# Mixture-of-experts chunks on one Trainium2 core: transposes set between products, and one bank exchanged

## The chip, the cores and the metric

The kernel runs on one core of a Trainium2 chip. The metric is the time on the device in microseconds, from the first to the last instruction plus what lies around them. The core's engines each run an instruction stream of their own and wait for each other through counters (semaphores): TensorE (PE in the rows; PEld are its weight loads), VectorE (DVE), ScalarE (ACT), GpSimd (POOL), and SyncE (SP), which issues most DMAs.

## The reference

Windowed attention gives 1536 rows of 512; a dense layer pair (2048 inner values) follows, then a gated layer of eight experts. Only the last is touched by the change:

```python
    expert_idx = np.argmax(logits, axis=1)          # E = 8 experts, N = 1536 tokens
    ...                                             # a token's place in its expert; capacity 384
    h = np.maximum(np.einsum('ecd,edf->ecf', disp, w1), 0.0)      # D = 512 -> F = 1024
    y = np.einsum('ecf,efd->ecd', h, w2)                          # F = 1024 -> D = 512
    ...
            out[i] = gate_w[i] * y[expert_idx[i], pos[i]]
```

With the inputs used here the experts get 715, 147, 16, 240, 4, 20, 277 and 117 tokens.

## The kernel before, in words

The order on every engine is the order in which the code is written (the schedule is manual). Attention, the dense pair and the routing take the first 420 us. The experts follow. An expert's tokens are handled in chunks of 128 rows, up to three (`NCH`), named (expert, chunk) below: (3,1) is the second chunk of expert 3. Chunk 0 of each expert always runs. Chunks 1 and 2 stand in nested conditionals (`guard`, `further_chunks`, L1310 to L1329), which each engine decides by a count that it reads itself. With these counts six further chunks run: (0,1), (0,2), (1,1), (3,1), (6,1), (6,2). Experts 2, 4, 5 and 7 skip theirs. An engine that skips a conditional raises its counter in one step by all that the body would have counted, and does so when its own earlier instructions are finished (the `EVENT_SEMAPHORE` of L1327 in the profile).

A chunk has four parts. All products are made of three matmuls, since every operand is split into a high and a low part (float32r).

- `turn_in` (L422): four transposes of the token rows into one PSUM bank, a copy to the high part on ACT (`xh`), a subtraction for the low part on DVE (`xl`).
- `expert_up` (L1253): two halves of 512 inner values, each 12 matmuls (128x512) into a bank of its own, and then the Relu of the half on ACT into `hh` (L1267).
- `turn_hidden` (L1270): for each half four transposes of `hh` (L1282), a copy to the high part on ACT (`hth`, L1285), a subtraction to the low part on DVE (`htl`, L1286). Between the two halves `between` transposes the tokens of the chunk after this one.
- `expert_down` (L1290): 24 matmuls over the eight blocks of inner values (high, high, low for each block), a scaling on DVE (`yo`, L1305), and a scatter by POOL.

The eight PSUM banks go round in three sets: three for transposes (`t`, rows name them es), three for `expert_up` (`u`, et), two for `expert_down` (`y`, et and eo). Each chunk (run or not) takes its banks when the program is built.

Weights for later experts are converted meanwhile: `expert_split` makes the high part by an ACT copy of 128x1024 (L1196, 1.05 to 1.07 us) and the low part by a DVE subtraction (L1197, 1.22 us). The loop over experts sets their places, and for experts of at least 1 it runs: `expert_up(e, 0)`, `turn_in(e + 1, 0)`, `turn_in(e, 1)`, splits, `expert_down(e - 1, 0)` (from expert 2 on), `turn_hidden(e, 0)`, further splits, `further_chunks(e, 1)`.

Of the kernel before, what the change touches and what calls it, by code (L numbers as in the profile page):

```python
# [9 lines left out]
F32 = mybir.dt.float32  # L10
F32R = mybir.dt.float32r
# [3 lines left out]
AF = mybir.ActivationFunctionType  # L15
ALU = mybir.AluOpType
# [19 lines left out]
def attention_mlp_moe_kernel(  # L36
# [17 lines left out]
    nc = tc.nc  # L54
    P = 128
    B, _, _, S = q.shape
    _, NG, _, GH, NQ, D1 = v.shape
# [4 lines left out]
    E = w_gate.shape[2]  # L62
    F = w1.shape[2]
    KD = DM // P
    KF = DFF // P
    KE = F // P
# [4 lines left out]
    if n_sink == 0 and window == 0:  # L71
# [4 lines left out]
    NCH = -(-max(1, min(capacity, NT)) // P)  # L76
# [8 lines left out]
    ident = const.tile([P, P], F32, name="ident")  # L85
# [6 lines left out]
        out=lt, in_=lt, pattern=[[1, P]], compare_op=ALU.is_gt, fill=0.0,  # L92
# [28 lines left out]
    def slot(tag, dt=F32R):  # L121
        slot_n[tag] = slot_n.get(tag, 0) + 1
        return slot_pool[tag].tile([P, SW], dt, tag=tag, name=f"{tag}_{slot_n[tag]}", bufs=1)
# [7 lines left out]
    for bl in range(NT // XB):  # L131
        for kp in range(KD // 2):
            for hl in range(2):
                t = slot(f"x{(bl * (KD // 2) + kp) * 2 + hl}")
# [167 lines left out]
    def spots(nb, seg):  # L302


        o = ns if nb == 1 and seg else 0
        offs = [o + n * BS for n in range(nb)]
        return offs, (0 if nb == 1 else P), offs[-1] + P
# [99 lines left out]
    three = ((0, 0), (0, 1), (1, 0))  # L407
# [5 lines left out]
    rows, tx, ep = {}, {}, []  # L413
# [9 lines left out]
    def turn_in(e, c, pt=None, th=None, tl=None):  # L423
        r = rows.pop((e, c))
        if pt is None:
            tag = "a" if c == 0 else "b"
            pt = next_bank("t")
            th = ep[0].tile([P, DM], F32R, tag=f"xh{tag}", name=f"xh{e}_{c}", bufs=1 + (c > 0))
            tl = ep[0].tile([P, DM], F32R, tag=f"xl{tag}", name=f"xl{e}_{c}", bufs=1 + (c > 0))
        for kk in range(KD):  # L430
            nc.tensor.transpose(pt[:, kk * P:(kk + 1) * P], r[:, kk * P:(kk + 1) * P], ident)
        nc.scalar.copy(th, pt)
        nc.vector.tensor_sub(tl, pt, th.bitcast(F32))
        tx[e, c] = (th, tl)
# [187 lines left out]
    with ExitStack() as actx:  # L622
# [12 lines left out]
        for n in range(QA):  # L635
            t = ap_c.tile([P, 2, S], F32, name=f"qa{n}")
# [5 lines left out]
        for i in range(NQ):  # L642
# [4 lines left out]
            offs, so, w = spots(len(row), seg)  # L647
# [4 lines left out]
            for (d, sink), o in zip(row, offs):  # L652
# [3 lines left out]
                if d * P - (P - 1) < 0:  # L656
                    nc.gpsimd.affine_select(
                        out=mb, in_=mb, pattern=[[-1, P]], compare_op=ALU.is_ge,
                        fill=NEG, base=d * P, channel_multiplier=1,
                    )  # L660
                if d * P + (P - 1) > window - 1:
                    nc.gpsimd.affine_select(
                        out=mb, in_=mb, pattern=[[1, P]], compare_op=ALU.is_ge,
# [9 lines left out]
        if small:  # L673
            for n in range(3):
                t = ap_c.tile([P, 2, 4, D1], F32, name=f"vsk{n}")
                nc.gpsimd.memset(t, 0.0)
                vsks.append(t)
                t = ap_c.tile([P, P], F32, name=f"pk{n}")
# [190 lines left out]
        for b in range(B):  # L869
            for hp in range(H // 2):  # L870
# [3 lines left out]
                for i0 in range(0, NQ, 2):  # L874
                    t = Item()
                    t.st, t.n, t.nm, t.units = st, len(groups), f"{st.nm}_{i0}", []
                    for ii in range(min(2, NQ - i0)):
                        u = Item()
# [32 lines left out]
        def at(xs, n):  # L911
            return xs[n] if 0 <= n < len(xs) else None
# [23 lines left out]
        for n in range(nu + 11):  # L936
            u = at(units, n)
# [36 lines left out]
            if n == nu - EARLY:  # L974
                nc.vector.tensor_scalar(
                    out=nalpha, in0=alpha_sb, scalar1=-1.0, scalar2=None, op0=ALU.mult
# [196 lines left out]
    experts = {}  # L1173
# [29 lines left out]
    def splits_to(n):  # L1203
        while split_n[0] < min(n, len(raw_src)):
            if split_n[0] == raw_n[0]:
                raw_loads()
            expert_split(split_n[0])
            split_n[0] += 1
# [27 lines left out]
    def next_bank(nm):  # L1236
        n = bank_n[nm] = bank_n.get(nm, -1) + 1
        return banks[nm][n % len(banks[nm])]
# [3 lines left out]
    counts, hid, hts = {}, {}, {}  # L1242
# [4 lines left out]
    def guard(e, c):  # L1247
        if e not in counts:
            counts[e] = nc.values_load(  # L1249
                cnt_i[0:1, e:e + 1], engines=GE, min_val=0, max_val=NT  # L1250
            )
        return tc.If(counts[e] > c * P)

    def expert_up(e, c):
        ups = experts[e][0]
        x = tx.pop((e, c))
        h = ep[0].tile([P, F], F32, tag="hh", name=f"hh{e}_{c}", bufs=1)
        for o in range(0, F, 512):
            ph = next_bank("u")
            for kk in range(KD):  # L1260
                for n, (xl, wl) in enumerate(((0, 0), (0, 1), (1, 0))):
                    nc.tensor.matmul(  # L1262
                        ph, x[xl][:, kk * P:(kk + 1) * P],
                        ups[kk][wl][:, o:o + 512],
                        start=(kk == 0 and n == 0), stop=(kk == KD - 1 and n == 2),
                    )
            nc.scalar.activation(h[:, o:o + 512], ph, AF.Relu)  # L1267
        hid[e, c] = h

    def turn_hidden(e, c, between=None):  # L1270
        h = hid.pop((e, c))


        tag = "b" if (c > 0) != (e == E - 1) else "a"
        th = ep[0].tile([P, F], F32R, tag=f"hth{tag}", name=f"hth{e}_{c}", bufs=1)
        tl = ep[0].tile([P, F], F32R, tag=f"htl{tag}", name=f"htl{e}_{c}", bufs=1)
        hts[e, c] = (th, tl)
        for o in range(0, F, 512):
            w = slice(o, o + 512)
            pt = next_bank("t")  # L1280
            for j in range(o // P, o // P + 4):
                nc.tensor.transpose(  # L1282
                    pt[:, j * P - o:(j + 1) * P - o], h[:, j * P:(j + 1) * P], ident
                )
            nc.scalar.copy(th[:, w], pt)  # L1285
            nc.vector.tensor_sub(tl[:, w], pt, th.bitcast(F32)[:, w])  # L1286
            if o == 0 and between:
                between()

    def expert_down(e, c):  # L1290
        downs = experts[e][1]
        ht = hts.pop((e, c))
        py = next_bank("y")
        n = e * NCH + c
        y = ep[0].tile([P, DM], F32, tag="yo", name=f"yo{n}", bufs=1)
        for j in range(KE):
            for x, (hl, wl) in enumerate(((0, 0), (0, 1), (1, 0))):
                nc.tensor.matmul(
                    py, ht[hl][:, j * P:(j + 1) * P], downs[j][wl],
                    start=(j == 0 and x == 0), stop=(j == KE - 1 and x == 2),  # L1300
                )
        if n == (E - 1) * NCH:
            nc.scalar.activation(y, py, AF.Copy, scale=meta[:, n, 0:1])
        else:
            nc.vector.tensor_scalar(  # L1305
                out=y, in0=py, scalar1=meta[:, n, 0:1], scalar2=None, op0=ALU.mult
            )
        nc.gpsimd.indirect_dma_start(  # L1308
            out=out[:, :], out_offset=bass.IndirectOffsetOnAxis(ap=token[:, n:n + 1], axis=0),
            in_=y, in_offset=None, bounds_check=NT - 1, oob_is_err=False,  # L1310
        )

    def further_chunks(e, c):

        if c == NCH:
            return
        if NCH > 3:
            for c in range(1, NCH):
                with guard(e, c):
                    if c > 1:  # L1320
                        fetch(e, c)
                        turn_in(e, c)
                    expert_up(e, c)
                    turn_hidden(e, c)
                    expert_down(e, c)
            return
        with guard(e, c):  # L1327
            expert_up(e, c)
            turn_hidden(e, c, (lambda: turn_in(e, c + 1)) if c + 1 < NCH else None)  # L1329
            expert_down(e, c)  # L1330
            further_chunks(e, c + 1)

    nc.gpsimd.dma_start(
        out=meta, in_=xs.rearrange("(n p) d -> p n d", p=P)[:, :, DM:XW]
# [4 lines left out]
    for e in range(E):  # L1339

        splits_to((e + 1) * PER - (e == 1))
        if e:
            expert_up(e, 0)
        raw_loads()
        if 0 < e < E - 1:
            turn_in(e + 1, 0)
        if e and NCH > 1:
            turn_in(e, 1)
        fetch(e + 2, 0)
        fetch(e + 1, 1)  # L1350
        splits_to((e + 1) * PER)
        raw_loads()
        splits_to((e + 1) * PER + PW1 + 1 * (e == 0) - (e == 1))
        if e == E - 1:
            turn_hidden(e, 0)
        if e >= 2:
            expert_down(e - 1, 0)
        if 0 < e < E - 1:
            turn_hidden(e, 0)
        if e == E - 1:  # L1360
            expert_down(e, 0)
        raw_loads()
        splits_to((e + 1) * PER + PW1)
        raw_loads()
        if e == 0:
            more = nc.values_load(more_i[0:1, 0:1], engines=GE, min_val=0, max_val=P)
            with tc.If(more > 0):
                turn_in(0, 0)
                expert_up(0, 0)
                turn_hidden(0, 0)  # L1370
                expert_down(0, 0)
            turn_in_slot(1, 0, "r4", next_bank("y"))
        further_chunks(e, 1)
        if NCH == 3:
            fetch(e + 1, 2)
# [64 lines left out]
```

## Time and profile before

| | |
|---|---|
| time, median of 3 runs | 606.62 us (605.58 to 607.24) |
| profiled execution | 605.23 us, of which the span from first to last instruction is 603.4 us |
| PE busy | 580.9 us, 96% of the span |
| DVE, ACT, POOL busy | 419.8, 346.6, 83.8 us |
| mean granted TensorE clock | 0.996 of full speed |

A timeline row gives the start of a group of instructions, its duration, engine, line, operation, output and inputs, tile shape and count; in brackets stands the idle time of the engine just before it and what ended that. Matmuls overlap, so the pace is read from one start to the next and not from the durations.

### The profile page before, as it was taken

To read this page: it belongs to the slowest core of one execution; us is meant where nothing else is said; L and a number is where in the kernel's file an instruction comes from. 1 tells how busy PE (TensorE), PEld (TensorE's weight loads), DVE (VectorE), ACT (ScalarE), POOL (GpSimd) and SP (SyncE) were. 2 spreads that over 40 slices of the span, in tenths; PEclk is the share of its full clock that TensorE was granted. 3 is DMA by queue.
4 is the path that set the end of the run, shared out by engine and by line. 5 is a ranking of instruction groups with operands and counts; after the bars stand their busy time and mean duration, and the time that the engine had idled before them with its cause. 6 is when DMAs were issued, how large, how long until landed. Compare 5 with 4: busy or idle time off the path is not lost. (4 is left out here: it accounts for less than half of the span.)

```text
span 603.4 us, 9071 instructions
## 1 busy us (share of the span) xinstructions
PE 580.9 (96%) x3174; PEld 485.2 (80%) x3174; DVE 419.8 (70%) x872; ACT 346.6 (57%) x641; POOL 83.8 (14%) x128
## 2 busy tenths in 40 slices
PE   7999999999989999999999999999999999999994
PEld 6999998878767888888899898976777777778783
DVE  6578878689999568974577787965326783885240
ACT  5677776566565545444466677854238474775330
POOL 5011433210000000000200021113210211111011
PEclk9999999999999999999999999999999999999998
DMA  7969742224641660000100022334918692993000
GB/s 226 329 209 307 209 142 71 71 70 145 200 146 68 216 272 2 0 1 0 54 19 2 0 78 74 113 110 136 348 45 295 216 380 102 348 356 127 18 21 35
DMA packets 32996, 83.86 MB, mean 139 GB/s; under 512 B 3646, under 2 KB 4206, under 8 KB 32944
## 3 DMA queue, kind: packets, MB, share of 16 engines
q1 hardware_dynamic: 28800, 71.66, 35.6%
q0 software_dynamic: 4144, 11.53, 5.5%
q8 instruction: 30, 0.49, 0.3%
q14 instruction: 22, 0.18, 0.1%
HBM read 68.75 MB, written 16.31 MB: 141 GB/s over the span
## 5 line engine op out<-in xcount | busy, mean ns | idle before, releaser
L362 PE MATMUL h<-x,r 128*128 128x512 f32 (+1 forms) x768 | 148.6, 340 | 3.2 <-DVE r L274 3.1
L362 PEld LDWEIGHTS h<-x,r 128*128 128x128 f32 x768 | 120.5, 189 | 22.8 <-DVE r L274 5.2
L393 PE MATMUL acc<-r,gh 128*128 128x512 f32 x384 | 120.5, 395 | 0.0
L393 PEld LDWEIGHTS acc<-r,gh 128*128 128x128 f32 x384 | 69.9, 188 | 14.2
L393 PE MATMUL acc<-r,gl 128*128 128x512 f32 x192 | 75.9, 395 | 0.0
L736 PE MATMUL s<-ka,qa 128*128 128x260 f32 x192 | 59.9, 399 | 4.2 <-DMA qa<-in_q_dram 3.9
L846 PEld LDWEIGHTS o<-vr,pT 128*128 128x128 f32 x352 | 55.5, 192 | 4.8
L375 DVE SCALAR_TENSOR_TENSOR g<-gn,nalpha,g 128x512 f32<-128x512 f32 (+1 forms) x64 | 39.4, 615 | 24.3 <-ACT g L374 24.2
L274 DVE TENSOR_TENSOR r<-wo,r 128x1024 fp32r<-128x1024 f32 x31 | 37.9, 1224 | 24.7 <-ACT r L271 24.5
L373 ACT ACTIVATE gn<-h 128x512 f32<-128x512 f32 (+1 forms) x64 | 31.4, 491 | 40.8 <-PE h L362 40.3
L846 PE MATMUL o<-vr,pT 128*128 128x65 f32 x352 | 53.6, 251 | 0.0
L1267 ACT ACTIVATE hh<-et 128x512 f32<-128x512 f32 x26 | 15.6, 599 | 65.5 <-PE et L1262 59.2
L1153 POOL DMA_INDIRECT xs<-x,slot_i x12 | 14.4, 1198 | 264.3 <-ACT g L374 164.4
L382 ACT CAST gh<-g 128x512 fp32r<-128x512 f32 (+1 forms) x64 | 32.9, 514 | 28.1 <-DVE g L375 27.9
L755 ACT ACTIVATE p<-sx,mn 128x260 f32<-128x260 f32 (+1 forms) x96 | 42.9, 488 | 9.4 <-DVE mn L751 8.9
L271 ACT CAST r<-wo 128x1024 fp32r<-128x1024 f32 (+1 forms) x33 | 33.8, 1025 | 22.6 <-PE acc L393 21.7
L768 PE MATMUL pt<-ident,p 128*128 128x128 f32 x176 | 46.5, 279 | 0.0
L751 DVE CUSTOM_DVE_ANT_0 sx<-s,mask 128x260 f32<-128x260 f32 (+1 forms) x96 | 36.9, 400 | 13.7 <-PE s L736 9.7
L393 PEld LDWEIGHTS acc<-r,gl 128*128 128x128 f32 x192 | 36.1, 188 | 8.6
L274 DVE TENSOR_TENSOR r<-wi,r 128x1024 fp32r<-128x1024 f32 x30 | 36.7, 1222 | 2.3 <-ACT r L271 2.3
L385 DVE TENSOR_TENSOR gl<-g,gh 128x512 fp32r<-128x512 f32 (+1 forms) x64 | 35.4, 553 | 1.6 <-ACT gh L382 1.6
L736 PEld LDWEIGHTS s<-ka,qa 128*128 128x128 f32 x192 | 30.9, 200 | 5.2 <-issue 3.8
(204 smaller groups left out, 1101.5 us busy)
## 6 DMA issues: line engine op xcount, KB each, us to landing
raw_all<-in_w_dram SPq DMA_DIRECT2D x36, 512.0 KB, 5.7
more_raw<-in_w_dram SPq DMA_DIRECT2D x28, 512.0 KB, 6.3
raw_all<-in_w_in_dram SPq DMA_DIRECT2D x8, 1024.0 KB, 6.3
raw_all<-in_w_out_dram SPq DMA_DIRECT2D x8, 1024.0 KB, 5.0
xs<-r SPq DMA_DIRECT2D x8, 771.0 KB, 10.1
rows<-xs POOLq DMA_DIRECT2D x20, 256.0 KB, 5.8
vr<-in_v_dram SPq DMA_DIRECT2D x4, 780.0 KB, 5.0
out_dram<-fill SPq DMA_DIRECT2D x2, 1536.0 KB, 13.2
```

Source lines behind the costliest of these rows:

```text
L271: nc.scalar.copy(hi[:, x], w[:, x])
L274: eng.tensor_sub(lo[:, x], w[:, x], hi.bitcast(F32)[:, x])
L362: nc.tensor.matmul(ph[:, :TB], wi[wl][:, kk, f0:f0 + P], xT_at(kk, tok, TB, xl), start=(n == 0), stop=(n == 3 * KD - 1),)
L375: nc.vector.scalar_tensor_tensor(out=g, in0=gn, scalar=nalpha[:, f:f + 1], in1=g, op0=ALU.mult, op1=ALU.add)
L382: nc.scalar.copy(gh, g)
L385: nc.vector.tensor_sub(gl, g, gh.bitcast(F32))
L393: nc.tensor.matmul(acc[t], g[a][:, t * P:(t + 1) * P], wo[w][:, f % FG, :], start=(f == 0 and x == 0), stop=(f == KF - 1 and x == 2),)
L736: nc.tensor.matmul(s[:, o:o + w], st.qa[:, h, toks], st.ka[:, c:c + w], start=True, stop=True, skip_group_check=True,)
L751: nc.vector.tensor_tensor_reduce(out=x[:, :w], in0=u.s[h][:, :w], in1=m[:, :w], scale=-scale, scalar=BIG, op0=ALU.add, op1=ALU.min, accum_ ...
L755: nc.scalar.activation(t.p[:, u.ii, h, :w], x[:, :w], AF.Exp, bias=t.mn[:, c:c + 1], scale=-1.0)
L768: nc.tensor.transpose(pt[:, c * P:(c + 1) * P], t.p[:, u.ii, h, u.offs[n]:u.offs[n] + P], ident,)
L846: nc.tensor.matmul(t.o[:, 2 * u.ii + h, :], u.pT[:, w], vr[:, hv * NQ + j, :], start=(not sg and n == 0), stop=(n == len(js) - 1), skip_gr ...
```

## The change

Three edits. First, a further chunk's work goes into one function, `chunk_alone`, which writes PE's instructions in another order: the transposes of the first half stand between the two halves of the second half's 12 `expert_up` matmuls, and the transposes of the second half stand after the first six `expert_down` matmuls. Second, the Relu of the second half is made in two pieces of 256 columns, one on ACT and one on DVE. Third, expert 1's `turn_in(1, 1)` takes a `y` bank in place of a `t` bank. Chunk 0 of every expert keeps the old functions; `put_out` is the end of `expert_down` under a name of its own.

```diff
@@ chunk_alone, new; further_chunks calls it for expert_up, turn_hidden, expert_down
+        mid = KD // 2
+        for o in cuts:
+            ph = next_bank("u")
+            up(o, ph, range(mid))
+            if o:
+                turn(o - 512)
+            up(o, ph, range(mid, KD))
+            if o < cuts[-1]:
+                nc.scalar.activation(h[:, o:o + 512], ph, AF.Relu)
+            else:
+                nc.scalar.activation(h[:, o:o + 256], ph[:, :256], AF.Relu)
+                nc.vector.tensor_scalar(
+                    out=h[:, o + 256:o + 512], in0=ph[:, 256:], scalar1=0.0, scalar2=None,
+                    op0=ALU.max,
+                )
+        if between:
+            between()
+        py = next_bank("y")
+        n = KE // 4
+        down(range(n))
+        turn(cuts[-1])
+        down(range(n, KE))
+        put_out(e, c, py)
...
-            expert_up(e, c)
-            turn_hidden(e, c, (lambda: turn_in(e, c + 1)) if c + 1 < NCH else None)
-            expert_down(e, c)
+            chunk_alone(e, c, (lambda: turn_in(e, c + 1)) if c + 1 < NCH else None)
             further_chunks(e, c + 1)
...
-            turn_in(e, 1)
+            turn_in(e, 1, next_bank("y") if e == 1 else None)
```

PE's order in chunk (3,1), before, from the last matmuls of `expert_up` on (`hh` is the Relu's output, `rows` the tokens of (3,2), `hth` and `htl` the parts that `expert_down` reads; the rows that are left out repeat the ones above them with other weights):

```order
L1262 MATMUL et_4694<-wi_3_5318,xl_1_5594 128x512
...
L1262 MATMUL et_4694<-wi_3_5322,xl_1_5594 128x512
L1282 MATMUL es_4691<-ident,hh_1_5682 128x128 [waits Activation_49]
L1282 MATMUL es_4691<-ident,hh_1_5682 128x128 x3
L431 MATMUL es_4692<-ident,rows_2_5536 128x128 [waits DMASW3_49,DVE_49]
L431 MATMUL es_4692<-ident,rows_2_5536 128x128 x3
L1282 MATMUL es_4693<-ident,hh_1_5682 128x128 [waits DVE_49,Activation_49]
L1282 MATMUL es_4693<-ident,hh_1_5682 128x128 x3
L1298 MATMUL et_4697<-x_4_5538,hth_1_5709 128x512 [waits Activation_49]
L1298 MATMUL et_4697<-x_4_5539,hth_1_5709 128x512
L1298 MATMUL et_4697<-x_4_5538,htl_1_5710 128x512 [waits DVE_49]
```

The same place in the change:

```order
L1330 MATMUL et_4694<-wi_3_5318,xl_1_5600 128x512
L1339 MATMUL es_4693<-ident,hh_1_5688 128x128 [waits Activation_49]
L1339 MATMUL es_4693<-ident,hh_1_5688 128x128 x3
...
L1330 MATMUL et_4694<-wi_3_5326,xl_1_5600 128x512
L432 MATMUL es_4691<-ident,rows_2_5542 128x128 [waits DMASW3_49,DVE_49]
L432 MATMUL es_4691<-ident,rows_2_5542 128x128 x3
L1348 MATMUL eo_4698<-x_4_5544,hth_1_5689 128x512 [waits Activation_49]
...
L1348 MATMUL eo_4698<-x_4_5544,htl_1_5690 128x512
L1339 MATMUL es_4692<-ident,hh_1_5688 128x128 [waits Activation_49]
L1339 MATMUL es_4692<-ident,hh_1_5688 128x128
L1339 MATMUL es_4692<-ident,hh_1_5688 128x128 [waits DVE_49]
```

The 12 transposes that stood together are now three groups of four with six matmuls between them, and the second half's transposes wait once for ACT's piece of the Relu and once for DVE's.

PE's first matmuls of expert 3's chunk 0 (`expert_up(3, 0)`, into bank et_4694), behind the conditionals of expert 2, before:

```order
L1327 UNCONDITIONAL_BRANCH
L1327 UNCONDITIONAL_BRANCH [waits PE_49] x2
L1262 MATMUL et_4694<-wi_3_5310,xh_0_5290 128x512 [waits Activation_49]
L1262 MATMUL et_4694<-wo_3_5311,xh_0_5290 128x512 [waits DVE_49]
L1262 MATMUL et_4694<-wi_3_5310,xl_0_5291 128x512
```

The same place in the change:

```order
L1391 UNCONDITIONAL_BRANCH
L1391 UNCONDITIONAL_BRANCH [waits PE_49] x2
L1263 MATMUL et_4694<-wi_3_5314,xh_0_5294 128x512 [waits DVE_49,Activation_49]
L1263 MATMUL et_4694<-wo_3_5315,xh_0_5294 128x512
L1263 MATMUL et_4694<-wi_3_5314,xl_0_5295 128x512
```

The bank was last read by the second Relu of chunk (2,1), which is now ACT's and DVE's, so the first matmul waits for a count of DVE too: that of the Relu piece L1364 inside the conditional (2,1). The second matmul's wait for an earlier count of DVE falls away. The same holds at the start of every expert from 2 on.

ACT's order from expert 1's token copies to chunk (1,1), before (`r` and `x` from `raw_all` or `more_raw` are the high parts of later weights):

```order
L432 CAST xh_1_5027<-es_4691 128x512 [waits DVE_49,PE_49]
L1196 CAST r_18_5039<-raw_all 128x1024 [waits DMAHW3_49]
...
L1285 CAST hth_0_5056<-es_4692 128x512 [waits DVE_49,PE_49]
L1285 CAST hth_0_5056<-es_4693 128x512 [waits DVE_49,PE_49]
L1196 CAST x_3_5073<-more_raw 128x1024 [waits DMAHW7_49]
L1249 TENSOR_LOAD cnt_i
L1327 COMPARE_AND_BRANCH
L1267 ACTIVATE hh_1_5092<-et_4696 128x512 [waits PE_49,Activation_49]
L1267 ACTIVATE hh_1_5092<-et_4694 128x512 [waits PE_49]
```

The same place in the change:

```order
L433 CAST xh_1_5029<-et_4697 128x512 [waits PE_49]
L1197 CAST r_18_5041<-raw_all 128x1024 [waits DMAHW3_49]
...
L1286 CAST hth_0_5058<-es_4691 128x512 [waits PE_49]
L1286 CAST hth_0_5058<-es_4692 128x512 [waits DVE_49,PE_49]
L1197 CAST x_3_5075<-more_raw 128x1024 [waits DMAHW7_49]
L1250 TENSOR_LOAD cnt_i
L1391 COMPARE_AND_BRANCH
L1361 ACTIVATE hh_1_5094<-et_4696 128x512 [waits PE_49,Activation_49]
L1342 CAST hth_1_5095<-es_4693 128x512 [waits DVE_49,PE_49]
L1363 ACTIVATE hh_1_5094<-et_4694 128x256 [waits PE_49]
```

The tokens' copy reads the other bank, and ahead of (1,1)'s first Relu ACT has the same copies in the same order.

## Rows read from the trace of the kernel before

**Rows 1.** The page: busy time of PE; granted clock in 40 slices, in tenths.

```profile
PE 580.9 (96%) x3174; PEld 485.2 (80%) x3174; DVE 419.8 (70%) x872; ACT 346.6 (57%) x641; POOL 83.8 (14%) x128
...
PEclk9999999999999999999999999999999999999998
```

**Rows 2.** PE's waits from 415 to 604 us: total, times, longest, us.

```profile
PE et L1262 <- ACTq L1327: 2.3, 3, 0.8
...
PE es L1282 <- ACT hh L1267: 0.5, 2, 0.3
```

**Rows 3.** Timeline of PE: expert 3's chunk 0, transposes and then matmuls, nothing waited for.

```profile
489.42 1.03 PE L431 MATMUL es<-ident,rows 128*128 128x128 f32 x8
...
490.76 0.40 PE L1298 MATMUL eo<-wi,htl 128*128 128x512 f32 x1
...
491.23 0.39 PE L1298 MATMUL eo<-wo,hth 128*128 128x512 f32 x1
```

**Rows 4.** Timeline of PE: chunk (3,1), transposes and the fourth matmul of the second product.

```profile
502.40 0.60 PE L1282 MATMUL es<-ident,hh 128*128 128x128 f32 x4
502.83 0.60 PE L431 MATMUL es<-ident,rows 128*128 128x128 f32 x4
...
504.79 0.63 PE L1298 MATMUL et<-x,hth 128*128 128x512 f32 x2
```

**Rows 5.** Timeline of PE: chunk (0,2), likewise.

```profile
440.39 0.60 PE L1282 MATMUL es<-ident,hh 128*128 128x128 f32 x4
441.24 0.66 PE L1282 MATMUL es<-ident,hh 128*128 128x128 f32 x4 [0.25 <-ACT hh L1267]
...
442.79 0.39 PE L1298 MATMUL eo<-wi,hth 128*128 128x512 f32 x1
```

**Rows 6.** Timeline of PE: chunk (0,1), likewise.

```profile
427.84 0.60 PE L431 MATMUL es<-ident,r 128*128 128x128 f32 x4
...
429.85 0.40 PE L1298 MATMUL et<-wi,hth 128*128 128x512 f32 x1
```

**Rows 7.** Timeline of PE and DVE: expert 1, ahead of chunk (1,1).

```profile
454.02 0.60 PE L1282 MATMUL es<-ident,hh 128*128 128x128 f32 x4
...
454.51 1.29 DVE L433 TENSOR_TENSOR xl<-es,xh 128x512 fp32r<-128x512 f32 x2 [3.58 <-issue]
...
455.25 0.66 PE L1282 MATMUL es<-ident,hh 128*128 128x128 f32 x4 [0.64 <-DVE xl L433]
...
456.08 0.49 PE L1262 MATMUL et<-wi,xh 128*128 128x512 f32 x1 [0.17 <-ACT r L1196]
```

**Rows 8.** Timeline of ACT: chunk (1,1).

```profile
459.53 1.08 ACT L1196 CAST x<-more_raw 128x1024 fp32r<-128x1024 f32 x1
460.48 0.63 ACT L1267 ACTIVATE hh<-et 128x512 f32<-128x512 f32 x1
462.00 0.60 ACT L1267 ACTIVATE hh<-et 128x512 f32<-128x512 f32 x1 [0.89 <-PE et L1262]
```

**Rows 9.** Timelines of PE and of DVE: chunk (1,1).

```profile
461.80 0.60 PE L1282 MATMUL es<-ident,hh 128*128 128x128 f32 x4
...
462.67 0.63 PE L1282 MATMUL es<-ident,hh 128*128 128x128 f32 x4
...
468.87 0.40 PE L1298 MATMUL et<-r,htl 128*128 128x512 f32 x1
...
463.11 0.69 DVE L1286 TENSOR_TENSOR htl<-es,hth 128x512 fp32r<-128x512 f32 x1 [0.26 <-ACT hth L1285]
```

**Rows 10.** Timeline, then L1327 by itself, 482 to 485.5 us: expert 2's skipped chunks.

```profile
483.36 1.28 DVE L1286 TENSOR_TENSOR htl<-es,hth 128x512 fp32r<-128x512 f32 x2
...
483.70 0.50 PE L1262 MATMUL et<-wi,xh 128*128 128x512 f32 x1 [0.77 <-ACTq L1327]
...
L1327 ACTq EVENT_SEMAPHORE  x1: 17/17/17, 483.6 to 483.6; - x1
...
L1327 DVEq EVENT_SEMAPHORE  x1: 21/21/21, 484.7 to 484.7; - x1
```

More of the change, by code (lines that the diff above doesn't have):

```diff
@@ L425, in turn_in @@
         if pt is None:
+            pt = next_bank("t")
+        if th is None:
             tag = "a" if c == 0 else "b"
-            pt = next_bank("t")
             th = ep[0].tile([P, DM], F32R, tag=f"xh{tag}", name=f"xh{e}_{c}", bufs=1 + (c > 0))
@@ L1268, in expert_up, with turn_hidden @@
         hid[e, c] = h
-    def turn_hidden(e, c, between=None):
+    def turn_hidden(e, c):
         h = hid.pop((e, c))
@@ L1286, in turn_hidden, with put_out @@
             nc.vector.tensor_sub(tl[:, w], pt, th.bitcast(F32)[:, w])
[L1287 to L1293, printed above, removed]
+    def put_out(e, c, py):
         n = e * NCH + c
         y = ep[0].tile([P, DM], F32, tag="yo", name=f"yo{n}", bufs=1)
[L1296 to L1301, printed above, removed]
         if n == (E - 1) * NCH:
@@ L1311, in expert_down, with chunk_alone, up, turn @@
         )
+    def expert_down(e, c):
+        downs = experts[e][1]
+        ht = hts.pop((e, c))
+        py = next_bank("y")
+        for j in range(KE):
+            for x, (hl, wl) in enumerate(((0, 0), (0, 1), (1, 0))):
+                nc.tensor.matmul(
+                    py, ht[hl][:, j * P:(j + 1) * P], downs[j][wl],
+                    start=(j == 0 and x == 0), stop=(j == KE - 1 and x == 2),
+                )
+        put_out(e, c, py)
+    def chunk_alone(e, c, between):
+        ups, downs = experts[e]
+        x = tx.pop((e, c))
+        h = ep[0].tile([P, F], F32, tag="hh", name=f"hh{e}_{c}", bufs=1)
+        tag = "b" if (c > 0) != (e == E - 1) else "a"
+        th = ep[0].tile([P, F], F32R, tag=f"hth{tag}", name=f"hth{e}_{c}", bufs=1)
+        tl = ep[0].tile([P, F], F32R, tag=f"htl{tag}", name=f"htl{e}_{c}", bufs=1)
+        three = ((0, 0), (0, 1), (1, 0))
+        cuts = list(range(0, F, 512))
+        def up(o, ph, ks):
+            for kk in ks:
+                for n, (xl, wl) in enumerate(three):
+                    nc.tensor.matmul(
+                        ph, x[xl][:, kk * P:(kk + 1) * P], ups[kk][wl][:, o:o + 512],
+                        start=(kk == 0 and n == 0), stop=(kk == KD - 1 and n == 2),
+                    )
+        def turn(o):
+            w = slice(o, o + 512)
+            pt = next_bank("t")
+            for j in range(o // P, o // P + 4):
+                nc.tensor.transpose(
+                    pt[:, j * P - o:(j + 1) * P - o], h[:, j * P:(j + 1) * P], ident
+                )
+            nc.scalar.copy(th[:, w], pt)
+            nc.vector.tensor_sub(tl[:, w], pt, th.bitcast(F32)[:, w])
+        def down(js):
+            for j in js:
+                for n, (hl, wl) in enumerate(three):
+                    nc.tensor.matmul(
+                        py, (th, tl)[hl][:, j * P:(j + 1) * P], downs[j][wl],
+                        start=(j == 0 and n == 0), stop=(j == KE - 1 and n == 2),
+                    )
+        mid = KD // 2
[12 more added lines that the diff above has]
+                    op0=ALU.max,
+                )
+        if between:
+            between()
+        py = next_bank("y")
+        n = KE // 4
+        down(range(n))
+        turn(cuts[-1])
+        down(range(n, KE))
+        put_out(e, c, py)
```

## The prediction

> **What bounds the kernel now.** I read the page first: PE is busy 96% of the span at a granted clock of nine tenths or more in all slices but the last [rows 1]. A kernel like that gains only where PE stands still, so the second view is PE's waits from the experts on (415 to 604 us). Two of its rows matter most: three waits of 0.8 us at the start of an `expert_up`, put down to ACT's sequencer at the conditional (L1327), and two for a Relu inside chunks [rows 2]. This view counts a wait from the modelled end of a matmul, and so hides waits that lie under that end. Hence the third view, PE's timeline read from start to start.
>
> The pace comes first. Where nothing is waited for, eight transposes and two matmuls take 490.76 - 489.42 = 1.34 us, and the next two matmuls 0.47 us [rows 3]; so a matmul takes 0.235 us, a transpose 0.108 us (four in 502.83 - 502.40 = 0.43 us [rows 4]), and 8 x 0.108 + 2 x 0.235 = 1.33 us: going from transposes to matmuls and back costs nothing by itself. This matters, because the change goes back and forth more often.
>
> **What the change removes.** In five of the six further chunks that run, PE has to wait between the last transposes and the fourth matmul of the second product. Eight transposes and three matmuls should take 0.86 + 0.70 = 1.57 us. They take 504.79 - 502.83 = 1.96 us in (3,1) [rows 4], so 0.39 us are lost; (6,1) repeats it to 0.01 us. In (0,1) they take 429.85 - 427.84 = 2.01 us [rows 6], 0.44 lost. In the two chunks that have no later tokens to transpose, PE stands between the halves until the Relu is done: 442.79 - 440.39 = 2.40 us in (0,2) [rows 5], 0.83 lost; (6,2) loses 0.82. Together 0.44 + 0.39 + 0.39 + 0.83 + 0.82 = 2.87 us.
>
> Are new waits put in their place? The first half's transposes come 6 x 0.235 = 1.41 us after that half's last product; a Relu of 0.60 us [rows 8] fits into that with 0.8 us over for its latencies, if ACT is free. For the second half, a turn takes from its first transpose to the end of the low part 463.11 + 0.69 - 461.80 = 2.00 us [rows 9], and this low part is first read 0.43 + 6 x 0.235 + 2 x 0.235 = 2.31 us after the turn begins: 0.3 us to spare. DVE's piece of the Relu waits for ACT's (its row in the order waits for ACT, not for PE), but both have 1.4 us of products to hide in. I take all 2.87 us as gained; at worst the low part is late in all six chunks and half of it stays.
>
> **What it costs in (1,1).** Here ACT isn't free. It works through copies for later weights, and the first Relu starts as soon as the copy that began at 459.53 lets it, at 460.48, ending at 461.11 [rows 8]. Before, nobody needed it until 461.80 [rows 9]. Now PE wants it after 18 matmuls. The bank exchange lets PE come early: the wait that kept it from 454.02 + 0.43 to 455.25 [rows 7] goes, and with it most of the branch that followed up to 456.08; but the third matmul reads the low part of the tokens, which DVE ends at 454.51 + 1.29 = 455.80. From about 455.87 on, 16 more starts bring PE to the turn at 459.63, where it waits until 461.11 + 0.07 = 461.18 (0.07 from the Relu's end, 462.00 + 0.60, to the transposes at 462.67 [rows 8, 9]). Behind this stand 12 transposes and 30 matmuls, 1.30 + 7.05 = 8.35 us, so the chunk ends at 469.53; before, it ended at 468.87 + 0.235 = 469.10. ACT's copies ahead of the Relu are the same and run back to back, so neither PE's early arrival nor the free bank moves them. **Cost 0.45 us**, and the bank exchange pays nothing.
>
> **What it costs where a chunk is skipped.** This is the largest new term. The first matmul of the next expert's `expert_up` writes the bank that the second Relu of chunk 1 reads. Before, ACT alone read it, and in a skipped chunk PE waited for ACT's counter: raised at 483.6, PE starts at 483.70 [rows 10]. Now DVE reads the bank too, so PE also waits for DVE's counter. If the chunk runs, DVE has long passed that point. If it is skipped, DVE raises its counter only behind its own earlier work, the low part of chunk 0, which ends at 483.36 + 1.28 = 484.64: raised at 484.7 [rows 10]. PE then starts at 484.64 + 0.11 = 484.75 (ACT's raise to PE is some 0.1), 1.05 us later than before. What is queued behind this matmul is all of PE's work for the next expert, and no other wait of PE in this stretch is long enough to absorb it. The skipped experts 2, 4 and 5 are the three waits of [rows 2]; expert 7 is skipped too, but nothing follows. 3 x 1.05 = 3.15 us, and since the order shows two waits on one matmul, a few hundredths for the second: **3.2 us** (bounds 3.1 and 3.4).
>
> The DMA side doesn't move: the number of loads, stores and scatters, and their queues, stay as they are, and a chunk's DVE work grows only by a 256-column piece that lies under six matmuls.
>
> **Sum.** -2.87 + 0.45 + 3.2 = +0.8 us. The profiled execution took 605.23 us, so this one would take 606.0; it lies 1.4 us under the median of the three runs, and on the median the change gives 606.62 + 0.8 = **607.4 us**, 0.13% more. I call less than 0.3% (1.8 us) no change, about what a measurement of this kernel can tell. So the forecast is "the same", made of a gain and a loss of about 3 us each.
>
> **Rivals.**
>
> - *The skipped chunks don't pay.* If DVE's count is met when the conditional is skipped (raised early, not behind `htl`), the 3.2 us vanish: -2.87 + 0.45 = -2.4, so 604.2 us, faster. For it speaks that nothing in the diff touches chunk 0; against it, that PE waited for ACT in just this way, three times out of three. It decides if DVE's raise comes before 483.7 in the place of [rows 10]. Chance 0.08.
> - *ACT is early enough in (1,1).* Then the chunk ends at 459.63 + 8.35 = 467.98, 1.1 us before 469.10: -2.87 - 1.1 + 3.2 = -0.8, so 605.8 us. Against it: back-to-back copies on ACT [rows 8]. Chance 0.09.
> - *Slower: the second half's low part comes late.* The 0.3 us to spare are worked out with a whole Relu on ACT; now the Relu, the next tokens' low part and this one queue on DVE behind each other. If DVE is over 0.3 us late, each of six chunks keeps a wait of 0.15 + 0.10 us or more: +0.8 + 1.5 = +2.3, so 608.9 us, slower. It decides from about 0.5 us of delay on. Chance 0.07.
> - *Slower: the clock falls.* The change makes four waits of PE of 1.5 to 1.9 us. The trace has none over 0.8 us in this stretch [rows 2] and the clock stayed at its upper level, 2.4 GHz [rows 1]. If it fell to 1.2 GHz behind them, the 24 matmuls that follow would take up to 24 x 0.235 = 5.6 us more at each; one such place is enough for 613 us. Chance 0.04. The Trainium skill's page "TensorE: Matmul & The Clock Gate" (section "HAM oscillation — how this bites in real kernels") states the rule: pauses of TensorE that are long enough bring the lower clock back, and each stretch of work then begins slow. By that rule the result would be the 613 us; no run here shows a pause of this length, so the trace neither agrees nor disagrees.
>
> **How the numbers follow.** The likeliest case has 0.72: 607.4, by its bounds (half of the 2.87 kept as a wait, 3.1 to 3.4 for the skips) 607.3 to 609.0, to which the spread of the runs comes (those of before lie 1.0 us under to 0.6 us over their median). The range of 605.6 to 609.0 takes in the second and third rival and leaves out the first and the clock. Of the likeliest case about a tenth lies over +1.8 us; with two thirds of the third rival and the clock that is 0.17 for slower. Faster is mostly the first rival: 0.08. The rest, 0.75, is the same.
>
> **What would show it.** In the profile after: the transposes' waits for `htl` and for the Relu gone from the six chunks, and second products at an even 0.235 us; in (1,1) a wait of PE of 1.5 us for the Relu, in the middle of `expert_up`; three waits at the start of `expert_up(3, 0)`, `(5, 0)` and `(6, 0)`, put down to DVE and 1.8 us long in place of 0.8; everything before 420 us as it was. The prediction is wrong if those three waits stay at 0.8 us, if new waits stand in front of the low parts, or if the granted clock drops there.

## The result, and the profile after

The changed kernel takes 609.99 us (median of 5 runs, 607.4 to 610.76); beside it on the same chip the kernel before took 605.99 us (5 runs, 605.48 to 607.24). The ratio is 1.0062, interval 1.0047 to 1.0077: 4.0 us slower. The forecast was 607.4 us, with 605.6 to 609.0 as range and "the same" as the likeliest outcome; the result lies 1 us above the range and on the slower side.

The profiled execution took 610.51 us, of which the span is 608.7. The page of the changed kernel, in the form of [rows 1]:

```profile
PE 581.3 (96%) x3174; PEld 487.2 (80%) x3174; DVE 422.9 (69%) x878; ACT 347.1 (57%) x641; POOL 83.1 (14%) x128
...
PEclk9999999999999999999999999999999999989998
```

PE does the same number of matmuls in about the same busy time. The new thing is in the clock: one slice near the end, the 36th, shows an 8 that [rows 1] doesn't have. A slice is 15 us long, so a dip of a few us in it barely shows; the page hides how it came about.

PE's waits of the changed kernel from 415 to 610 us (total, times, longest), which answer to [rows 2]. L1263 is the matmul of `expert_up`, L1339 the transposes in `chunk_alone`:

```profile
PE et L1263 <- ACT x L1197: 3.8, 2, 1.9
PE et L1263 <- ACT wi L1197: 1.9, 1, 1.9
PE es L1339 <- ACT hh L1361: 1.3, 1, 1.3
PE et L1263 <- PEq L1391: 1.1, 2, 0.5
```

The three waits of 0.8 us at the skipped chunks have become three of 1.9 us, and the transposes' short waits of [rows 2] have gone, except for one new wait of 1.3 us for a Relu, which is in (1,1). The view puts the three down to ACT's weight copies. That is a wrong name: in the program's order the matmul waits for ACT and DVE, and DVE's raise is the one that comes just before it, as the next rows show. PE's timeline at the skip of expert 2, which answers to [rows 10]:

```profile
482.32 1.03 PE L1283 MATMUL es<-ident,hh 128*128 128x128 f32 x8
485.27 0.47 PE L1263 MATMUL et<-wi,xh 128*128 128x512 f32 x1 [1.91 <-ACT x L1197]
...
486.04 0.59 PE L1263 MATMUL et<-wi,xh 128*128 128x512 f32 x1
486.43 0.63 PE L1263 MATMUL et<-wo,xh 128*128 128x512 f32 x1
486.86 0.63 PE L1263 MATMUL et<-wi,xl 128*128 128x512 f32 x1
...
489.42 0.44 PE L1263 MATMUL et<-wi,xl 128*128 128x512 f32 x1
489.69 0.39 PE L1263 MATMUL et<-wi,xh 128*128 128x512 f32 x1
489.92 0.40 PE L1263 MATMUL et<-wo,xh 128*128 128x512 f32 x1
```

and in the same stretch DVE's timeline, and then the skipped conditional's line (now L1391) by itself, with the raises of the counters (count, duration in ns, first and last start):

```profile
483.79 1.27 DVE L1287 TENSOR_TENSOR htl<-es,hth 128x512 fp32r<-128x512 f32 x2
```
```profile
L1391 ACTq EVENT_SEMAPHORE  x1: 17/17/17, 484.1 to 484.1; - x1
...
L1391 DVEq EVENT_SEMAPHORE  x1: 21/21/21, 485.1 to 485.1; - x1
```

ACT's counter is up at 484.1, DVE's only at 485.1, behind its `htl`, and PE starts at 485.27. That is the wait that was forecast. What follows it was not. From one start to the next the matmuls take 486.86 - 486.43 = 0.43 us until 489.42, and 0.23 us again from 489.69 on. The windows of PE (length, PE busy and count, granted clock as a share, DMA share, GB/s) give the clock by stretch: the pause, the slow stretch, the work behind it, and then the same three places at the skip of expert 5, with that of expert 4 (528.20) between them:

```profile
483.00:485.20 2.20, 0.36 (x4) 1.00 1.04 406
486.10:489.70 3.60, 3.60 (x11) 0.53 1.05 349
489.70:495.00 5.30, 5.30 (x28) 1.00 1.00 366
528.20:532.00 3.80, 3.79 (x16) 1.00 1.00 379
543.30:544.40 1.10, 1.07 (x4) 0.86 1.00 387
544.40:547.60 3.20, 3.20 (x9) 0.51 0.89 272
```

TensorE's granted clock was at its upper level, 2.4 GHz, in the pause and for about a microsecond of work after it, and then fell to 0.53 and 0.51, the lower level of 1.2 GHz, for some three microseconds. It did so behind two of the three pauses, which are equally long (1.91, 1.91 and 1.92 us in the timeline's brackets).

**Where the time went.** The first matmuls of the `expert_up` of each stage, read from the two timelines of PE, divide the span. The difference is that of the lengths, changed less before:

| stage | start before | start after | length changes by |
|---|---|---|---|
| all ahead of (0,1) | 0 | 0 | +0.93 |
| (0,1) | 421.83 | 422.76 | -0.19 |
| (0,2) | 434.77 | 435.51 | -0.82 |
| expert 1's chunk 0 | 447.70 | 447.62 | -1.10 |
| (1,1) | 456.08 | 454.90 | +1.65 |
| expert 2's chunk 0, with its skip | 469.68 | 470.15 | +1.10 |
| expert 3's chunk 0 | 483.70 | 485.27 | +1.53 |
| (3,1) | 496.70 | 499.80 | -0.30 |
| expert 4's chunk 0, with its skip | 510.28 | 513.08 | +1.10 |
| expert 5's chunk 0, with its skip | 524.31 | 528.21 | +1.10 |
| expert 6's chunk 0 | 538.33 | 543.33 | +1.49 |
| (6,1) | 551.35 | 557.84 | -0.40 |
| (6,2) | 564.35 | 570.44 | -0.82 |
| expert 7 and the end | 577.28 | 582.55 | +0.03 |

The five chunks give 2.53 us, (1,1) with the stage ahead of it costs 0.55, the three skips 3.30, the two stages behind a fallen clock 3.02. With 0.93 ahead of all experts this is 5.3 us, the difference of the spans (608.7 and 603.4). That is more than the 4.0 us between the medians: each profile is one execution, and the 0.93 lies ahead of every edited instruction.

The fourth of the waits shown above hides a small cost that the prediction didn't have. It stands where PE leaves the conditionals of a chunk that ran, at the first matmul behind (1,1) and behind (3,1). Before, the row was:

```profile
PE et L1262 <- PEq L1327: 0.8, 2, 0.4
```

In the timelines each of these two waits is 0.42 us before and 0.53 us in the changed kernel. It is 0.53 in the third and fourth experiments below too, where DVE also reads the bank that the next expert writes first, and 0.42 in the six others, where it doesn't. So the matmul's second counter seems to cost 0.11 us even where DVE is long past its piece; that rests on which kernels show it, and no run isolates it.

In the chunks the new order does what it says. PE's timeline of the changed kernel in (3,1), which answers to [rows 4], and the place where (1,1) waits, to [rows 9]:

```profile
459.41 0.39 PE L1330 MATMUL et<-wi,xl 128*128 128x512 f32 x1
461.10 0.66 PE L1339 MATMUL es<-ident,hh 128*128 128x128 f32 x4 [1.29 <-ACT hh L1361]
461.51 0.48 PE L1330 MATMUL et<-wi,xh 128*128 128x512 f32 x1
...
505.92 0.60 PE L432 MATMUL es<-ident,rows 128*128 128x128 f32 x4
506.28 0.71 PE L1348 MATMUL eo<-x,hth 128*128 128x512 f32 x2
506.83 0.39 PE L1348 MATMUL eo<-x,htl 128*128 128x512 f32 x1
507.06 0.62 PE L1348 MATMUL eo<-x,hth 128*128 128x512 f32 x2
```

In (3,1) four transposes and three matmuls take 507.06 - 505.92 = 1.14 us, which is 4 x 0.108 + 3 x 0.235: nothing is lost. In (1,1) PE is ready at 459.41 + 0.235 = 459.65 and starts at 461.10, behind ACT, whose timeline answers to [rows 8]:

```profile
459.46 1.08 ACT L1197 CAST x<-more_raw 128x1024 fp32r<-128x1024 f32 x1
460.41 0.64 ACT L1361 ACTIVATE hh<-et 128x512 f32<-128x512 f32 x1
```

### The profile page after: what moved, and what is told of

Its sections match the earlier page's. It is cut to its first block, busy times and chain, and to the rows that moved or that the text cites. A ratio compares the mean times of both kernels' runs of the same rounds, so it can differ in the third digit from the quotient of the medians.

```text
span 608.7 us, 9079 instructions
## 1 busy us (share of the span) xinstructions
PE 581.3 (96%) x3174; PEld 487.2 (80%) x3174; DVE 422.9 (69%) x878; ACT 347.1 (57%) x641; POOL 83.1 (14%) x128
## 5 line engine op out<-in xcount | busy, mean ns | idle before, releaser
L769 PEld LDWEIGHTS pt<-ident,p 128*128 128x128 f32 x176 | 32.2, 183 | 2.4 <-ACT p L756 0.3
```

Source lines behind the costliest of these rows:

```text
L769: nc.tensor.transpose(pt[:, c * P:(c + 1) * P], t.p[:, u.ii, h, u.offs[n]:u.offs[n] + P], ident,)
```

## The experiments

The theory after this reading: (a) DVE as a second reader of the bank that the next expert writes first costs 1.1 us at each skip, and (b) the longer pauses let the clock fall, about 1.5 us each time it does; the new order itself is a gain. The rivals: the new order costs time through something that the timeline doesn't show, or the clock falls for a reason that has nothing to do with the pauses. Times stand beside runs of the kernel before on the same chip: 605.77 us (18 runs) for the first four experiments, 605.76 us (17 runs) for the last four.

**1. The second Relu whole on ACT.** The order and the bank exchange stay, and DVE no longer reads the bank.

```diff
-            if o < cuts[-1]:
-                nc.scalar.activation(h[:, o:o + 512], ph, AF.Relu)
-            else:
-                nc.scalar.activation(h[:, o:o + 256], ph[:, :256], AF.Relu)
-                nc.vector.tensor_scalar(
-                    out=h[:, o + 256:o + 512], in0=ph[:, 256:], scalar1=0.0, scalar2=None,
-                    op0=ALU.max,
-                )
+            nc.scalar.activation(h[:, o:o + 512], ph, AF.Relu)
```

> The second edit alone is undone: both Relus of a further chunk stay whole on ACT, the rest is the change. Theory A (the loss is DVE's share in the bank that the next expert's first matmul writes: three pauses of PE of about 2.1 us at the skipped experts, and a clock that falls behind some of them): the pauses go back to about 0.95 us from start to start beyond the pace, no stretch runs below a granted clock of 1.00, and the time is 605.99 - 2.87 + 0.45 = 603.6 us, about 0.4% below before. Theory B (the new order of PE's work is what loses, by the clock or by waits of its own): stretches of half clock stay, and the time stays between 607 and 610 us.

Measured: 603.2 us (9 runs, 602.18 to 605.25), ratio 0.9964, interval 0.9951 to 0.9976. PE's waits in this kernel, the same stretch:

```profile
PE et L1263 <- ACTq L1384: 2.3, 3, 0.8
PE es L1339 <- ACT hh L1360: 1.3, 1, 1.3
```

The three waits are back at 0.8 us and named as in [rows 2], and with them 6.8 us are gone. That is more than twice the 3.3 us of the waits themselves; the two falls of the clock, 3.0 us, are most of the rest. The new order is a gain of 2.6 us once it doesn't bring these waits along.

**2. The two banks of a further chunk 1 exchanged.** The second half's bank, which DVE reads, is then not the one that the next expert writes first. DVE's piece of the Relu stays.

```diff
-        for o in cuts:
-            ph = next_bank("u")
+        phs = [next_bank("u") for o in cuts]
+        if c == 1:
+            phs.reverse()
+        for o, ph in zip(cuts, phs):
```

> Everything of the change is kept, DVE's piece of the Relu too; only the two up banks of chunk 1 are exchanged, so that the bank that DVE reads there is not the one that the next expert's first matmul writes. Theory A: as with the Relu on ACT, 603.6 us within 0.5, three pauses of the old length, no half clock. If DVE's piece of the Relu itself costs (its place in DVE's queue, or late low parts), the time stays clearly above that of the Relu on ACT, by 0.2 us a chunk or more (1.2 us over six).

Measured: 607.92 us (5 runs, 606.39 to 608.33), ratio 1.0035, interval 1.0022 to 1.0048. A miss, and an instructive one. PE's waits in this kernel, and below them its timeline at chunk (0,1):

```profile
PE et L1330 <- ACTq L1432: 2.5, 1, 2.5
PE et L1263 <- ACTq L1393: 2.3, 3, 0.8
```
```profile
424.73 7.09 PE L1330 MATMUL et<-x,r 128*128 128x512 f32 x18 [2.54 <-ACTq L1432]
431.67 0.60 PE L1339 MATMUL es<-ident,hh 128*128 128x128 f32 x4
```

At the three skips the wait is 0.8 us, as meant. But (0,1)'s first matmul now writes a bank that ACT reads in a conditional ahead of it, `more`, which this run skips too, and so waits 2.54 us for ACT's raise there. Its first 18 matmuls take 431.67 - 424.73 = 6.94 us, where 18 x 0.235 = 4.2 would do. PE's windows in the empty stretch, the slow part and the work behind it:

```profile
422.20:424.70 2.50, 0.00 (x0) 0.81 1.00 353
425.30:430.40 5.10, 5.10 (x13) 0.50 1.07 301
430.40:434.00 3.60, 3.60 (x21) 0.98 0.98 382
```

The granted clock is 0.50 behind this pause, and 0.81 in the mean of the pause itself: it fell before PE went on. The trap is the same, with another engine at another conditional, and so is what follows it.

**3. DVE's piece alone, in the kernel before.** The old order, the old banks, and only the split of the second Relu.

```diff
-            nc.scalar.activation(h[:, o:o + 512], ph, AF.Relu)
+            if c == 0 or o == 0:
+                nc.scalar.activation(h[:, o:o + 512], ph, AF.Relu)
+            else:
+                nc.scalar.activation(h[:, o:o + 256], ph[:, :256], AF.Relu)
+                nc.vector.tensor_scalar(
+                    out=h[:, o + 256:o + 512], in0=ph[:, 256:], scalar1=0.0, scalar2=None,
+                    op0=ALU.max,
+                )
```

> The kernel before with one thing added: in further chunks the second Relu is split between ACT and DVE, in the old order of PE's work. Theory A: three longer pauses, 3 x 1.14 = 3.4 us, some 0.2 us more in each of the two chunks without later tokens, and the clock falling behind the pauses in some runs at 1.5 us each: 609.6 to 614 us. Theory B: the order is the old one, so the clock doesn't fall and the time is at most 609.8 us, with no spread beyond that of before (1.8 us).

Measured: 612.17 us (4 runs, 611.0 to 612.7), ratio 1.0104, interval 1.0089 to 1.0119. The largest loss of all, from the smallest edit. PE's waits in it, and then its windows behind the three skips:

```profile
PE et L1262 <- ACT x L1196: 3.8, 2, 1.9
PE et L1262 <- ACT wi L1196: 1.9, 1, 1.9
```
```profile
486.00:490.00 4.00, 4.00 (x17) 1.00 0.99 343
529.20:532.10 2.90, 2.90 (x8) 0.50 1.01 357
546.30:549.20 2.90, 2.90 (x8) 0.51 0.90 265
```

The same three pauses stand here without the new order, and again two of three have a fallen clock behind them: here behind the second and the third, in the changed kernel behind the first and the third. Three times 1.1 and two times 1.5 us are 6.3 of the 6.4 us that it loses.

**4. The pauses filled.** The changed kernel, with five matmuls more, whose result nobody reads, ahead of `expert_up(e, 0)` where the three pauses are. They write another `u` bank, one that DVE doesn't read.

```diff
+        if e in (3, 5, 6):
+            for _ in range(5):
+                nc.tensor.matmul(
+                    banks["u"][1], tx[e, 0][0][:, :P], experts[e][0][0][0][:, :512],
+                    start=True, stop=True,
+                )
         if e:
             expert_up(e, 0)
```

> The change, with five extra matmuls (128x512, results overwritten) ahead of the first product of experts 3, 5 and 6, in a bank that only ACT reads: PE works through the second half of each long pause and waits for DVE only after that. The three experts begin about as late as in the change. Theory A with pauses as the cause of the clock: no stretch below 1.00 at these places, all runs near 605.99 - 2.87 + 0.45 + 3.4 = 607.0 us, spread as before (1.8 us). If the clock falls for another cause (DMA load, the order), it still falls there in some runs, and the runs reach 608.5 to 611 us.

Measured: 607.38 us (9 runs, 606.49 to 607.47), ratio 1.0025, interval 1.0015 to 1.0035. PE's timeline at the first of the three places, and the windows behind all of them:

```profile
484.00 1.46 PE L1406 MATMUL et<-wi,xh 128*128 128x512 f32 x5 [0.77 <-ACTq L1391]
485.30 0.40 PE L1263 MATMUL et<-wi,xh 128*128 128x512 f32 x1
```
```profile
484.00:490.00 6.00, 6.00 (x26) 1.00 1.01 364
525.40:531.40 6.00, 5.91 (x25) 1.00 0.95 349
540.60:546.60 6.00, 5.92 (x25) 1.00 0.91 315
```

`expert_up` starts no earlier than in the changed kernel (485.30 beside 485.27): the wait is there in full, and only the emptiness is gone. With it go the falls, 609.99 - 607.38 = 2.6 us of the median, and most of the spread, which was 3.4 us from lowest to highest and is now 1.0. The filling has a small price of its own: counted from the first matmul of the stage before, `expert_up` starts 0.17, 0.13 and 0.06 us later than in the changed kernel. This tells theory (b) from its rival: the clock falls because PE stands still there.

**5. The banks exchanged from expert 1 on.** As the second experiment, without the place where that one fell into the trap.

```diff
-        if c == 1:
+        if c == 1 and e > 0:
```

> As the run with exchanged up banks, but from expert 1 on; chunk (0,1) keeps the banks of the change, since in that run its first matmul had come to wait for the skipped conditional ahead of it. DVE's piece of the Relu stays in all six chunks. Theory A (only the bank matters): the time of the Relu on ACT, 603.2 us within 0.5; pauses of the old length at experts 3, 5 and 6; no half clock. If DVE's piece costs by itself: 604.4 us or more.

Measured: 602.77 us (5 runs, 602.54 to 602.95), ratio 0.9949, interval 0.9937 to 0.9962. The skips' waits are 0.8 us each here too. So DVE's piece of the Relu costs nothing by itself: with it 602.77, without it (the first experiment) 603.2, and the runs of the two overlap. What cost was which bank it reads. Beside the second experiment 5.15 us are gone. At (0,1) the profiles show 2.3 us of pause (its first matmul starts 3.19 us after the transposes ahead of it there, and 0.93 here) and 2.7 us of slow matmuls behind it.

**6. The third edit alone,** in the kernel before: `turn_in(1, 1)` in a `y` bank.

```diff
...
-            turn_in(e, 1)
+            turn_in(e, 1, next_bank("y") if e == 1 else None)
```

> The kernel before with the third edit alone: expert 1's second tokens are turned in a bank of expert_down. PE's wait of 0.80 us in front of the second half's transposes goes, and the branch behind it (0.33 us) is hidden, but the third matmul of (1,1) waits some 0.3 + 0.1 us for the tokens' low part, and the first transposes some 0.1 us for the Relu: 0.6 us gained, 605.2 us against 605.8. The rival, that ACT's Relu eats all of it here too, gives 605.8.

Measured: 605.5 us (11 runs, 604.62 to 606.21), ratio 0.9997, interval 0.9988 to 1.0006. The wait of [rows 7] for `xl` is gone from the list of waits, but the interval runs from -0.7 to +0.4 us (0.9988 and 1.0006 times 605.76): the expected 0.6 lies in it, and so does no change at all. By the times it can't be told. The two profiles show a little: from the first matmul of expert 1's chunk 0 to that of expert 2's, PE takes 469.68 - 447.70 = 21.98 us in the kernel before and 469.51 - 447.87 = 21.64 us here, 0.34 less.

**7. The first experiment with the third edit undone.** The code shows what differs from the first experiment.

```diff
-            turn_in(e, 1, next_bank("y") if e == 1 else None)
+            turn_in(e, 1)
```

> The Relu whole on ACT and the new order, but the third edit undone: expert 1's second tokens in a t bank again. By my sum the Relu of (1,1) sets when PE goes on, whatever PE did ahead of it: 603.2 us as with the edit, within 0.3, the 0.8 us wait back in front of (1,1) and the wait for the Relu inside it shorter by about as much as was lost ahead. If the bank edit pays in the new order: 603.9 to 604.3 us.

Measured: 603.26 us (6 runs, 602.19 to 604.4), ratio 0.9960, interval 0.9947 to 0.9973, the same as the first experiment. Its waits of PE:

```profile
PE es L1283 <- DVE xl L434: 0.6, 1, 0.6
PE es L1339 <- ACT hh L1360: 0.6, 1, 0.6
```

The wait for `xl` is back at 0.6 us and the one for the Relu has shrunk from 1.3 to 0.6: the exchange of the bank only moves PE's waiting from ahead of (1,1) into it, since ACT sets the time at which the Relu ends. From expert 1's first matmul to expert 2's it takes 22.43 us in the profiles of both, with the exchange and without it.

**8. The old order in (1,1) alone,** all else as in the first experiment.

```diff
...
-            chunk_alone(e, c, (lambda: turn_in(e, c + 1)) if c + 1 < NCH else None)
+            if (e, c) == (1, 1):
+                expert_up(e, c)
+                turn_hidden(e, c, lambda: turn_in(e, c + 1))
+                expert_down(e, c)
+            else:
+                chunk_alone(e, c, (lambda: turn_in(e, c + 1)) if c + 1 < NCH else None)
```

> The Relu whole on ACT, the new order in every further chunk but (1,1), which keeps the old order; the bank edit stays. If the wait for the Relu inside (1,1) is what the new order costs there, this gains 0.45 + 0.6 = 1.0 us over the Relu on ACT alone: 602.2 us against 603.2. If it costs nothing, 603.2 or, with the old order's own waits, 603.6 us.

Measured: 602.22 us (5 runs, 601.8 to 602.54), ratio 0.9939, interval 0.9926 to 0.9952. The fastest kernel of the study, 3.5 us under the kernel before and 1.0 under the first experiment. PE no longer waits for the Relu in (1,1); what is left there is this row among its waits:

```profile
PE eo L1311 <- DVE htl L1287: 0.3, 1, 0.3
```

So with ACT's copies in front, 24 products make a better cover for the first Relu than 18. The stretch from expert 1's first matmul to expert 2's takes 21.66 us, as in the sixth experiment (21.64) and not as in the first (22.43). With the old order the exchanged bank seems to pay its 0.34 us, since PE's early start isn't lost again; no run has this kernel without the exchange.

## Why the prediction was wrong

The step that failed is the rival "the clock falls", in its chance (0.04) and in its price (5.6 us at each place). I held the fall unlikely because the trace of before showed none, but its longest pause in this stretch was 0.8 us [rows 2]: it said nothing about 1.9. So the sum had no term for the clock. The fall came behind two of the three pauses in the profiled execution, and the fourth experiment, which fills the pauses and changes nothing else, shows that they cause it and that it costs 2.6 us of the median, or 3.0 with the 0.36 that the filling adds. The price was too high because I let all 24 matmuls of the `expert_up` run slow. Between 486.43 and 489.42 there are seven steps of 0.43 us, not 24, and the stage grows by 1.5 us. The rival had 613 us from one such place; two places made 3.0 us.

The trace of before holds a stretch that could have warned of the fall and of its size, though not in the part that I read. PE's first eight matmuls of the span (L736, 128x260), behind 3.9 us without work, start (7.47 - 3.87) / 8 = 0.45 us apart; four of the same shape from 7.89 on take 0.95 us, 0.24 each. By these rows the slow start costs some 1.7 us and then ends. But the granted clock reads 1.00 there, so it is not shown that the clock is what makes it slow.

The Trainium skill's page "TensorE: Matmul & The Clock Gate" (section "HAM oscillation — how this bites in real kernels") gave the direction rightly: work after a pause of TensorE runs slow. The trace agrees (granted clock 0.53 and 0.51), at pauses shorter than the waits in the page's example. The section ties the fall to waits longer than any of these pauses, so by it alone they would have brought none; the runs decide, and four of six pauses of 1.9 us had a fall behind them. The 613 us that the prediction puts down to the rule came from my 24 slow matmuls and not from the page.

The other steps, in the order of the prediction:

- *The waits removed in the chunks, 2.87 us.* Right in kind, 2.53 measured. (0,2) and (6,2) gave 0.82 each, as predicted to 0.01, and (6,1) 0.40. (0,1) gave 0.19 in place of 0.44: its first 18 matmuls take 427.20 - 422.76 = 4.44 us, and 4.21 and 4.19 in the first and fifth experiments, so the loss lies ahead of the transposes that were moved; its cause is open. (3,1) gave 0.30 in place of 0.39; all its matmuls after the transposes run evenly, and the missing tenth is the 0.11 us by which the wait at its end has grown.
- *(1,1), 0.45 us.* Measured 0.55. (The prediction's own two ends, 469.53 and 469.10, give 0.43.) PE was ready at 459.65 (predicted 459.63) and went on at 461.10 (461.18); here too 0.11 us is the longer wait at the end. The statement that the exchange of the bank pays nothing is borne out by the first and seventh experiments (22.43 us with and without it), with the limit that the sixth and eighth put to it: it pays nothing as long as (1,1) has the new order.
- *The skipped chunks, 3.2 us.* Measured 3.30: DVE's counter is raised behind `htl`, ACT's has been up for 1.0 us. From the end of `htl` to PE's start 485.27 - 485.06 = 0.21 us pass, where the prediction had 0.11 and a few hundredths for the second counter. The first experiment takes the term away, the third makes it alone, the second makes its like at another conditional.
- *The sum* was +0.8. The same terms as measured give -2.53 + 0.55 + 3.30 = +1.3, and without falls of the clock the changed kernel takes 607.38 (fourth experiment), 1.6 us more than the kernel before on the same chip, of which 0.36 is the filling. So the forecast of 607.4 was that of a kernel whose clock stays up. That the two numbers meet is luck: the forecast was half a microsecond short in its terms and stood on a median of three runs, 606.62, which the larger sets put at 605.8 to 606.0.
- *The chances.* The terms that the prediction names for "slower" add up to 0.16, not 0.17; nothing hangs on it.
- *What was to be seen.* The three waits grew to 1.9 us as predicted, but named after ACT, not DVE. "Everything before 420 us as it was" was off by 0.93 us. Of these 0.76 are one wait for a DMA near 396 us, ahead of every edit. In the profiles of the first and fifth experiments the same matmul starts 0.7 and 0.9 us earlier than in the changed kernel, in the third as late; why it varies stays open.

The three pauses are alike, and yet the clock fell behind two of them, not the same two in two kernels. What picks them is open; no run here tells it apart. One of the changed kernel's five runs took 607.4 us, close to the profiled 610.51 less two falls (3.0 us); without a trace of that run it stays a guess that it had none. Its mean granted clock doesn't speak for the guess: 0.994, the same as in the run of 609.99 us.

## What to carry to other kernels

A second engine that reads part of a PSUM bank becomes a second counter that the bank's next writer must wait for, and where the read stands in a skipped conditional that counter is raised only when its engine has come to the skip behind its own earlier work (DVE 1.0 us after ACT here): before splitting a read, ask which bank it is, who writes it next, and when each engine reaches the skip. A new pause of PE costs its length and may cost nearly that much again through the clock, so a trace without long pauses is no evidence about them, and if the wait can't go, work that fills it saves the second half. And an order that spreads transposes between products shortens the cover of the first Relu: where the engine of that Relu has other work in front of it, the old order is the better one.

## What the runs showed of the hardware that was not expected

The fall and the pause aren't aligned. In the changed kernel the clock was at full speed through the pause (1.00 from 483.00 to 485.20) and for about a microsecond of work, then at 0.53 for some three microseconds of dense matmuls, then at full speed again. In the second experiment it fell inside the pause, and the slow stretch behind it lasted to about 430.4, over five microseconds of work. Among the seven pauses of 1.9 us and more from 415 us on (three in the changed kernel, three in the third experiment, one in the second) five had a slow stretch behind them. PE's last work before each of them was transposes, eight at the skips and four in the second experiment, and no run varies that. Behind the waits of 1.3 us in (1,1) and of 0.8 us at the skips the profiles show none.
